# Weights times v in an attention and two-layer kernel: the second head's matmul goes first in each turn of the two heads

## The chip, the cores and the metric

One core of a Trainium2 chip runs the whole program. The metric is the device time of one execution in microseconds. An execution that was recorded by the profiler gives the rows that are shown below; its own time stands beside the times of the runs without a profile.

## What is computed

The reference is attention with a causal mask and a bias from cumulated gates, followed by two feed-forward layers:

```python
scores = scale * q @ k.T                       # 4 batches, 8 heads, 576 positions, 64 wide
bias = -(cum[:, None] - cum[None, :])          # cum: running sum of max(s, 0)
scores = where(causal, -1e9, scores + minimum(bias, 0))
attn = exp(scores - max(scores)); attn = attn / (sum(attn) + 1e-9)
x = attn @ v                                   # then (2304, 512)
x = max(x @ w1, x @ w2, x @ w3) @ w_out        # 512 -> 768 -> 512
x = ((x @ w_a) * (x @ w_b)) @ w_out2           # 512 -> 1536 -> 512
```

The change touches `attn @ v` alone. Everything is float32.

## The kernel before

Two heads are worked on together as a pair, and the 576 query positions of a batch are cut into a part of 256 (R = 0) and one of 320 (R = 1). That gives 4 x 2 x 4 = 32 pairs. For each pair the scores go to PSUM, VectorE adds the mask and finds the maximum (line 367), ScalarE takes the exponential (line 374), GpSimd divides by the sum (line 383), and TensorE transposes the weights in pieces of 128 x 128 (`f_t0` at line 476 for R = 0; `t_unit` and `t_joint` at lines 512, 514 and 525 for R = 1). ScalarE copies the transposes from PSUM into the tile `PF` (lines 479, 517, 520, 526), whose second index is the head.

Then `f_pv` (lines 481 to 502) multiplies by v. The result of a pair is one PSUM tile `fpv` of 128 partitions: the first head writes partitions 0 to 63, the second 64 to 127. Each matmul has a stationary operand of 128 x 64, so the first head's matmuls use columns 0 to 63 of the array and the second head's columns 64 to 127. For R = 0 each head has two matmuls, of 256 and 128 columns; for R = 1 it has five, of 320, 320, 320, 192 and 64. They are float32, and in the trace each stands as two records of that many columns. The list `mm` holds them by head, and the loop at lines 495 and 496 takes one of each head in turn. ScalarE and VectorE then read the tile (`f_x`, lines 506 and 507) and write `Xh` and `Xl`, the input of the first feed-forward layer. All 32 sets of matmuls together are called the 32 groups below: 16 shorter ones (R = 0) and 16 longer ones (R = 1).

The order on each engine is not the order in the code. The program is written as a stream of small pieces (pieces of attention, units of the first feed-forward layer `gate` at line 553 and `outp` at line 580, weight loads `load_w1`), each with a priority (`tc.high_priority`). A scheduler then plans the program with times of its own and puts on an engine what has the priority among those instructions that it holds to be ready. So a matmul of line 498 whose operand it holds to be late is passed by others, such as gates of the first layer. Instructions on TensorE are executed in the order that the scheduler wrote. The second feed-forward layer (line 951) follows from 530 us on and has no part in the attention.

The copy of the second head's transposes comes last in a pair: `f_t0` is called for head 0 and then head 1 (line 667), and in R = 1 the last piece is `do_t(2, 1)` (line 689).

Of the kernel before, what the change touches and what calls it, by code (L numbers as in the profile page):

```python
# [27 lines left out]
def kernel(  # L28
# [175 lines left out]
    def pt4(t, h):  # L204
        return t[:, h].rearrange("p (j c) -> p j c", c=N1)
# [275 lines left out]
    def f_pv(R, PF, vn):  # L481
        n = Q0 if R == 0 else N1
        ps = ps_t.tile([P, 512], F32, tag="t", name="fpv")
        mm = []
        for h in range(2):
            hs = slice(h * D, h * D + D)
            if R == 0:
                m = [(vn[:, 0, hs], PF[:, h, 0:256], 0), (vn[:, 1, hs], PF[:, h, 256:384], P)]
            else:
                m = [(vn[:, j, hs], pt4(PF, h)[:, j], 0) for j in range(3)]  # L490
                m.append((vn[:, 3, hs], pt4(PF, h)[:, 3, P:], P))
                m.append((vn[:64, 4, hs], PF[:64, h, 3 * N1 : 3 * N1 + 64], 256))
            mm.append(m)

        for t in range(len(mm[0])):
            for h in range(2):
                w, x, c0 = mm[h][t]
                nc.tensor.matmul(  # L498
                    ps[h * D : h * D + D, c0:n], w, x,
                    start=(t == 0), stop=(t == len(mm[h]) - 1),  # L500
                )
        return ps
# [129 lines left out]
    def attn_pieces(i, X):  # L632
# [10 lines left out]
        def pv():  # L643
            f_x(R, p, f_pv(R, st["PT"], nat_of.pop(i)[2]), *X())
            ahead(i + 2)
# [643 lines left out]
```

## Time and profile before

| what | value |
|---|---|
| median of 3 runs | 975.48 us (974.85 to 976.46) |
| the profiled execution's own time | 977.47 us |
| its span, from the first to the last instruction | 975.7 us |
| TensorE (PE) busy | 927.9 us, 95% of the span |
| VectorE busy | 618.5 us, 63% |
| ScalarE busy | 397.7 us, 41% |
| GpSimd busy | 276.6 us, 28% |
| line 498 on PE | 73.7 us busy in its largest group of instructions, 432 records |

The table has one execution. Busy time of PE counts a matmul from its start to its modelled end; since matmuls overlap in the array, the distance from one start to the next tells what an instruction costs, and the views in order of time give the starts. A row in order of time that ends in x18 holds 18 instructions that follow each other.

### The profile page before, as it was taken

The page shows a single profiled execution, that of the slowest core. Times are in us where ns is not written, and L with a number is a line of the kernel's source. Part 1 is how long each engine was busy: PE and PEld are TensorE (multiplying, and loading weights), DVE is VectorE, ACT ScalarE, POOL GpSimd, SP SyncE. Part 2 cuts the span into 40 slices and gives each one's busy share as a digit, 9 for nine tenths or more (in the row PEclk, how much of TensorE's full clock was granted, in tenths as well). Part 3 has the DMA queues.
Part 4 walks back from the last instruction along what each step waited for, and adds up shares of the span by engine and source line. Part 5 has one row for each costly group of instructions (what it writes and reads, how often), then busy time and mean ns, then how long its engine had stood idle before and what let it go on. Part 6 is the DMA issues. An engine that isn't in the chain of part 4 may idle for free.

```text
span 975.7 us, 17008 instructions
## 1 busy us (share of the span) xinstructions
PE 927.9 (95%) x6182; PEld 849.9 (87%) x6182; DVE 618.5 (63%) x1404; ACT 397.7 (41%) x902; POOL 276.6 (28%) x379
## 2 busy tenths in 40 slices
PE   5899999999999999999999789999999999599998
PEld 4576689988998889988889789999999999599998
DVE  5999623544344543454291888887877579868774
ACT  4766733555446554465431422232322233233231
POOL 6676522232233222333241212111111111212210
PEclk9999999999999999999999979999999999799999
DMA  5555241313223132220130524444443121552531
GB/s 168 191 183 164 89 107 53 92 39 103 57 79 91 40 91 68 80 81 29 60 115 22 195 76 135 151 152 151 145 136 100 57 98 57 159 169 89 172 109 44
DMA packets 55211, 102.34 MB, mean 105 GB/s; under 512 B 5736, under 2 KB 39432, under 8 KB 55128
## 3 DMA queue, kind: packets, MB, share of 16 engines
q1 hardware_dynamic: 55128, 101.26, 32.9%
q8 instruction: 49, 0.80, 0.4%
q14 instruction: 34, 0.28, 0.1%
HBM read 77.29 MB, written 23.94 MB: 104 GB/s over the span
## 4 chain that ended last, share of the span: by engine, by line
PE 66%; DVE 13%; DMA 13%; issue 3%; POOL 1%; ACT 1%; SPq 1%; POOLq 0%; DVEq 0%; ACTq 0%
PE g L553 20%; PE X L951 14%; PE Z L951 7%; PE o L580 7%; PE fpv L498 6%; PE Y L951 3%; DMA wraw<-in_moe_w_out_dram 3%; PE t L512 2%; DVE u L838 2%; DMA wraw<-in_moe_w_b_dram 2%; DVE wl L838 2%; PE s L390 1%; DMA qvraw<-in_qv_dram 1%; PE s L391 1%; DMA wraw<-in_moe_w_a_dram 1%
## 5 line engine op out<-in xcount | busy, mean ns | idle before, releaser
L553 PE MATMUL g<-Xh,hg 128*128 128x256 f32 (+1 forms) x576 | 174.5, 305 | 4.0 <-ACT xo L585 2.4
L553 PE MATMUL g<-Xl,hg 128*128 128x256 f32 (+1 forms) x576 | 174.4, 303 | 0.9 <-DVE rs L378 0.9
L553 PE MATMUL g<-Xh,lg 128*128 128x256 f32 (+1 forms) x576 | 174.2, 303 | 0.0
L553 PEld LDWEIGHTS g<-Xh,hg 128*128 128x128 f32 x576 | 109.3, 190 | 9.6 <-issue 3.3
L553 PEld LDWEIGHTS g<-Xl,hg 128*128 128x128 f32 x576 | 109.8, 191 | 4.0 <-issue 2.1
L553 PEld LDWEIGHTS g<-Xh,lg 128*128 128x128 f32 x576 | 109.7, 191 | 4.0 <-issue 3.5
L951 PE MATMUL X<-xh,wh 128*128 128x384 f32 x288 | 99.3, 345 | 7.5 <-ACT u L986 3.0
L86 POOL TENSOR_SCALAR wh<-wval 128x256 fp32r<-128x256 f32 x84 | 43.7, 531 | 200.4 <-PE Z L951 128.2
L951 PE MATMUL X<-xl,wh 128*128 128x384 f32 x288 | 97.9, 340 | 1.0 <-DVE xl L838 1.0
L951 PE MATMUL X<-xh,wl 128*128 128x384 f32 x288 | 98.0, 340 | 0.3 <-DVE wl L838 0.3
L951 PE MATMUL X<-woh,slot 128*128 128x256 f32 x432 | 83.0, 285 | 6.8 <-ACT slot L79 6.3
L562 DVE TENSOR_TENSOR hf<-g,hf 128x256 f32<-128x256 f32 (+1 forms) x96 | 43.6, 455 | 64.0 <-PE g L553 53.5
L838 DVE TENSOR_TENSOR slot<-hraw,slot 128x768 fp32r<-128x768 f32 x63 | 63.1, 1024 | 21.7 <-POOL slot L86 18.7
L951 PEld LDWEIGHTS X<-woh,slot 128*128 128x128 f32 x432 | 69.7, 193 | 7.3 <-ACT slot L79 6.7
L498 PE MATMUL fpv<-PF,qvraw 128*64 128x320 f32 (+4 forms) x432 | 73.7, 376 | 0.0
L383 POOL TENSOR_SCALAR P<-P,rs 128x128 f32<-128x128 f32 (+2 forms) x80 | 48.9, 616 | 71.2 <-DVE rs L379 47.8
L90 POOL TENSOR_TENSOR hl<-hf,hh 128x256 fp32r<-128x256 f32 (+1 forms) x48 | 40.7, 847 | 98.7 <-ACT hh L79 98.4
L951 PEld LDWEIGHTS X<-xh,wh 128*128 128x128 f32 x288 | 54.5, 189 | 12.1 <-ACT u L986 3.9
L86 POOL TENSOR_SCALAR slot<-hraw 128x768 fp32r<-128x768 f32 x27 | 27.3, 1010 | 129.5 <-DVE hraw L838 54.8
L374 ACT ACTIVATE P<-P,nm 128x128 f32<-128x128 f32 (+2 forms) x80 | 46.4, 581 | 38.1 <-DVE nm L367 34.8
L951 PE MATMUL X<-wol,slot 128*128 128x256 f32 x216 | 61.3, 285 | 0.0
L498 PEld LDWEIGHTS fpv<-PF,qvraw 128*64 128x64 f32 (+1 forms) x432 | 32.7, 137 | 31.6 <-issue 13.0
(158 smaller groups left out, 2370.1 us busy)
## 6 DMA issues: line engine op xcount, KB each, us to landing
hT<-u SPq DMA_DIRECT2D x72, 192.0 KB
hraw<-hT SPq DMA_DIRECT2D x36, 384.0 KB
wraw<-in_moe_w_dram SPq DMA_DIRECT2D x18, 512.0 KB
wraw<-in_moe_w_out_dram SPq DMA_DIRECT2D x18, 512.0 KB
qvraw<-in_qv_dram SPq DMA_DIRECT2D x12, 640.0 KB
kraw<-in_kT_dram SPq DMA_DIRECT2D x24, 288.0 KB
wraw<-in_moe_w_a_dram SPq DMA_DIRECT2D x12, 512.0 KB
wraw<-in_moe_w_b_dram SPq DMA_DIRECT2D x12, 512.0 KB
```

What stands on the lines that cost most here:

```text
L86: nc.gpsimd.tensor_scalar(o, i, scale, 1.0, op0=ALU.mult, op1=ALU.mult)
L90: e.tensor_tensor(o, a, b, op=ALU.subtract)
L374: nc.scalar.activation(pt[:, c0:c1], pt[:, c0:c1], AF.Exp, bias=first, scale=-1.0, accum_out=sm[:, g : g + 1],)
L383: nc.gpsimd.tensor_scalar(pt[:, c0:c1], pt[:, c0:c1], rs[:, g : g + 1], 1.0, op0=ALU.mult, op1=ALU.mult,)
L390: nc.tensor.matmul(ps, QA1[:, qs], KB1[:, h, ksl], start=True, stop=False)
L498: nc.tensor.matmul(ps[h * D : h * D + D, c0:n], w, x, start=(t == 0), stop=(t == len(mm[h]) - 1),)
L512: nc.tensor.transpose(ps[:, j * P : j * P + P], pt[:, j * P : j * P + P], ident)
L553: nc.tensor.matmul(ps[:, :n], w[:, kk, :], x[:, kk, :], start=(i == 0), stop=(i == len(mm) - 1),)
L562: nc.vector.tensor_tensor(hf, ps[:, :n], hf, op=ALU.max)
L580: nc.tensor.matmul(ps[:, :n], w[:, c, :], x[:, m, :n], start=(i == 0), stop=(i == len(mm) - 1),)
L838: {"V": nc.vector, "P": nc.gpsimd}[e].tensor_tensor(o, a, b, op=op)
L951: nc.tensor.matmul(ps[:, :n], w, x, start=(first and i == 0), stop=(i == len(mm) - 1), skip_group_check=not first,)
```

## The change

In the loop of `f_pv` over the two heads, the second head's matmul of each turn is written ahead of the first head's:

```diff
         for t in range(len(mm[0])):
-            for h in range(2):
+            for h in (1, 0):
                 w, x, c0 = mm[h][t]
                 nc.tensor.matmul(
                     ps[h * D : h * D + D, c0:n], w, x,
                     start=(t == 0), stop=(t == len(mm[h]) - 1),
                 )
```

An empty line is added above the loop, so each line behind it has a number higher by one in the changed kernel (498 becomes 499, 553 becomes 554). The matmuls, their operands and their results are the same 224 as before. What changes is the order that the scheduler writes.

The first place is TensorE at a longer group late in the attention, `fpv_5355`. Before, around the group's first matmul (`t2` is a transpose of the second head's weights, `g` a gate matmul of the first layer):

```order
L553 MATMUL g_5195<-Xh_4466,hg_1_1_124 128x256
L553 MATMUL g_5195<-Xl_4467,hg_1_1_124 128x256
L512 MATMUL t2_5334<-ident_81,P2_5292 128x128 x3
L498 MATMUL fpv_5355<-PF_5174,qvraw_4938 64x320
L553 MATMUL g_5195<-Xh_4466,lg_1_1_125 128x256
L553 MATMUL g_5195<-Xh_4466,hg_1_1_124 128x256
L553 MATMUL g_5195<-Xl_4467,hg_1_1_124 128x256
```

and 23 rows later the rest of the same group (`s3` are scores of the next pair):

```order
L553 MATMUL g_5261<-Xh_4466,hg_0_2_128 128x256
L553 MATMUL g_5261<-Xl_4467,hg_0_2_128 128x256
L498 MATMUL fpv_5355<-PF_5174,qvraw_4938 64x320 x5
L498 MATMUL fpv_5355<-PF_5174,qvraw_4938 64x192 x2
L498 MATMUL fpv_5355<-PF_5174,qvraw_4938 64x64 x2
L390 MATMUL s3_5447<-KB1_112,QA1_114 128x512
```

Now the whole group stands in one place:

```order
L554 MATMUL g_5245<-Xh_4466,lg_2_1_127 128x256
L554 MATMUL g_5245<-Xh_4466,hg_2_1_126 128x256
L499 MATMUL fpv_5355<-PF_5174,qvraw_4938 64x320 x6
L499 MATMUL fpv_5355<-PF_5174,qvraw_4938 64x192 x2
L499 MATMUL fpv_5355<-PF_5174,qvraw_4938 64x64 x2
L390 MATMUL s3_5447<-KB1_112,QA1_114 128x512
L391 MATMUL s3_5447<-KB2_113,QA2_115 128x512
```

The group's first matmul, the first head's, stood apart from the other nine; now all ten follow each other, at the place where the nine stood, ahead of the same scores.

The second place is a shorter group, `fpv_4619`, on TensorE. Before (`s0` are scores of a later pair):

```order
L553 MATMUL g_4476<-Xl_3667,hg_0_1_122 128x320
L498 MATMUL fpv_4619<-PF_4491,qvraw_4312 64x256
L553 MATMUL g_4476<-Xh_3666,lg_0_1_123 128x320
L390 MATMUL s0_4680<-KB1_112,QA1_114 128x256
L553 MATMUL g_4476<-Xh_3666,hg_0_1_122 128x320
L391 MATMUL s0_4680<-KB2_113,QA2_115 128x256
L553 MATMUL g_4476<-Xl_3667,hg_0_1_122 128x320
L390 MATMUL s0_4680<-KB1_112,QA1_114 128x256
L553 MATMUL g_4476<-Xh_3666,lg_0_1_123 128x320
L391 MATMUL s0_4680<-KB2_113,QA2_115 128x256
L553 MATMUL g_4510<-Xh_3666,hg_1_1_124 128x320
L498 MATMUL fpv_4619<-PF_4491,qvraw_4312 64x256
```

Now:

```order
L554 MATMUL g_4510<-Xl_3667,hg_1_1_124 128x320
L554 MATMUL g_4510<-Xh_3666,lg_1_1_125 128x320
L499 MATMUL fpv_4619<-PF_4491,qvraw_4312 64x256 x2
L499 MATMUL fpv_4619<-PF_4491,qvraw_4312 64x128 x2
L554 MATMUL g_4510<-Xh_3666,hg_1_1_124 128x320
L554 MATMUL g_4510<-Xl_3667,hg_1_1_124 128x320
```

One matmul of 256 columns stood nine rows ahead of the other three; now the four stand together.

The third place is the start of the program, around `fpv_446` on TensorE (`ft0` are transposes of the next pair, `f2`, `f3` scores of later ones). Before:

```order
L553 MATMUL g_928<-Xh_273,hg_0_0_116 128x256
L553 MATMUL g_972<-Xh_273,hg_1_0_118 128x256
L498 MATMUL fpv_446<-PF_373,kqv_172 64x256 x2
L498 MATMUL fpv_446<-PF_373,kqv_172 64x128 x2
L553 MATMUL g_928<-Xl_274,hg_0_0_116 128x256
L553 MATMUL g_928<-Xh_273,lg_0_0_117 128x256
```

Now:

```order
L554 MATMUL g_986<-Xh_273,lg_2_0_121 128x256
L499 MATMUL fpv_446<-PF_373,kqv_172 64x256
L476 MATMUL ft0_510<-ident_81,F0_463 128x128
L476 MATMUL ft0_515<-ident_81,F0_479 128x128
L476 MATMUL ft0_510<-ident_81,F0_463 128x128
L499 MATMUL fpv_446<-PF_373,kqv_172 64x256
L476 MATMUL ft0_515<-ident_81,F0_479 128x128
L476 MATMUL ft0_510<-ident_81,F0_463 128x128
L499 MATMUL fpv_446<-PF_373,kqv_172 64x128
L476 MATMUL ft0_515<-ident_81,F0_479 128x128
L499 MATMUL fpv_446<-PF_373,kqv_172 64x128
L434 MATMUL f2_560<-kraw_277,qvraw_278 128x384
```

Here the group was in one piece, and now transposes stand between all of its four matmuls.

Over the whole program, the groups stand so on TensorE (a piece is a row of line 498's matmuls with nothing between them):

| | groups in one piece | in two | in three | in four | in five | pieces in all |
|---|---|---|---|---|---|---|
| before | 2 | 27 | 2 | 1 | 0 | 66 |
| now | 28 | 0 | 1 | 2 | 1 | 44 |

Before, the two whole groups are `fpv_446` and `fpv_1962`, those in three pieces `fpv_650` and `fpv_787`, and that in four `fpv_1811`. Now four of the first five groups are in pieces: `fpv_268` in three, `fpv_446` and `fpv_528` in four, `fpv_650` in five; `fpv_359` and all groups from the sixth on stand whole. From `fpv_1962` on, the kernel before has 12 longer groups and 8 shorter ones in two pieces each. In the second layer a few short stretches of matmuls change places with their neighbours.

## Rows read from the trace of the kernel before

**Rows 1.** Busy us by stretch: length, PE, PEld, DVE, ACT, POOL; then clock, DMA share, GB/s.
```profile
0.00:50.00 50.00, 37.35 (x176) 26.54 (x176) 37.07 (x106) 29.90 (x77) 31.69 (x44) 0.97 0.60 179
50.00:100.00 50.00, 47.52 (x304) 34.12 (x303) 47.15 (x105) 34.00 (x76) 34.91 (x32) 1.00 0.52 165
...
150.00:485.00 335.00, 334.15 (x2413) 298.23 (x2412) 146.85 (x486) 168.13 (x420) 99.02 (x144) 1.00 0.23 66
485.00:600.00 115.00, 103.87 (x606) 100.20 (x605) 83.81 (x148) 33.05 (x64) 29.06 (x40) 0.94 0.32 108
```

**Rows 2.** All waits of PE from 150 to 485 us: engine, line, releaser, us, times, longest.
```profile
PE ft L476 <- POOL P L383: 0.4, 2, 0.2
```

**Rows 3.** PE in order of time at 453 us: start us, us, what runs.
```profile
453.17 0.60 PE L512 MATMUL t<-ident,P 128*128 128x128 f32 x4
...
453.73 0.28 PE L553 MATMUL g<-Xh,lg 128*128 128x256 f32 x1
```

**Rows 4.** PE in order of time around a longer group, 442 to 450 us.
```profile
442.77 0.49 PE L512 MATMUL t<-ident,P 128*128 128x128 f32 x3
443.19 0.75 PE L498 MATMUL fpv<-PF,qvraw 128*64 128x320 f32 x2
443.87 0.39 PE L553 MATMUL g<-Xh,lg 128*128 128x256 f32 x1
444.09 0.28 PE L553 MATMUL g<-Xh,hg 128*128 128x256 f32 x1
...
447.01 2.42 PE L498 MATMUL fpv<-PF,qvraw 128*64 128x320 f32 x18
449.35 0.50 PE L390 MATMUL s<-KB,QA 128*128 128x512 f32 x1
```

**Rows 5.** PE in order of time around a shorter group, 377 to 381 us.
```profile
377.32 0.31 PE L553 MATMUL g<-Xh,hg 128*128 128x320 f32 x1
377.47 0.31 PE L553 MATMUL g<-Xl,hg 128*128 128x320 f32 x1
377.71 0.65 PE L498 MATMUL fpv<-PF,qvraw 128*64 128x256 f32 x2
378.28 0.41 PE L553 MATMUL g<-Xh,lg 128*128 128x320 f32 x1
378.54 0.28 PE L390 MATMUL s<-KB,QA 128*128 128x256 f32 x1
...
379.69 0.86 PE L498 MATMUL fpv<-PF,qvraw 128*64 128x256 f32 x6
380.48 0.42 PE L553 MATMUL g<-Xl,hg 128*128 128x320 f32 x1
```

**Rows 6.** PE in order of time at 157 us, a shorter group in one piece.
```profile
157.25 0.87 PE L498 MATMUL fpv<-PF,qvraw 128*64 128x256 f32 x8
158.05 0.41 PE L553 MATMUL g<-Xh,hg 128*128 128x320 f32 x1
```

**Rows 7.** PE in order of time, 142 to 145 us, a shorter group in four pieces.
```profile
141.95 0.31 PE L553 MATMUL g<-Xh,hg 128*128 128x320 f32 x1
142.19 0.65 PE L498 MATMUL fpv<-PF,qvraw 128*64 128x256 f32 x2
...
145.35 0.31 PE L553 MATMUL g<-Xh,lg 128*128 128x320 f32 x1
```

**Rows 8.** Waits of PE up to 150 us.
```profile
PE f L434 <- DMA kraw<-cs: 9.3, 1, 9.3
PE g L553 <- ACT Xh L79: 1.6, 1, 1.6
...
PE f L434 <- DMA kraw<-ck: 1.1, 2, 0.7
```

**Rows 9.** ScalarE in order of time: the second head's copy before the body of rows 4.
```profile
443.43 0.45 ACT L517 COPY PF<-t 128x384 f32<-128x384 f32 x1
```

**Rows 10.** Tile fpv, weight loads: count, then ns shortest/median/longest.
```profile
L498 PEld LDWEIGHTS fpv<-PF,qvraw x432: 128/136/230, 22.3 to 481.0; 128*64 128x64 f32 x123, 64*64 64x64 f32 x21
```

## Prediction

> **What bounds the kernel now.** I read the busy time by stretch first. From 150 to 485 us PE is busy 334.15 of 335.00 us, at a granted clock of 1.00 (its 2.4 GHz level), while DVE has 146.85, ACT 168.13 and POOL 99.02 us of work and the DMA engines are busy 23% of the time [rows 1]. The view of PE's waits agrees: 0.4 us in all of that stretch [rows 2]. So there the time is what TensorE's instructions cost one after the other, and an instruction that leaves its queue shortens the run by its whole cost. The start is different: in the first 100 us PE is busy 37.35 + 47.52 us, DVE is busy 37.07 and 47.15 us [rows 1], and apart from 9.3 us before the first matmul PE waits another 15.1 - 9.3 = 5.8 us, 1.6 us of them at one place [rows 1, 8]. From 485 to 600 us PE lacks 115.00 - 103.87 = 11.1 us [rows 1].
>
> Then I read PE in order of time, since busy times overlap and only the distance from one start to the next is a cost.
>
> **What a piece costs.** The order of the changed kernel shows that the change does one thing to nearly all groups: the first head's first matmul, which stood apart, goes back to its group. Two prices are needed, that of the piece where it stands and that of the same matmul inside the group.
>
> *Longer group, standing apart.* From the first of three transposes (442.77) over the piece (443.19) to the second gate behind it (444.09) are 1.32 us [rows 4]. Without a piece, four transposes and the first gate take 453.73 - 453.17 = 0.56 us [rows 3]; a fourth transpose adds 0.60 - 0.49 = 0.11 us [rows 3, 4], so three take 0.45 us. The piece costs 1.32 - 0.45 = 0.87 us.
>
> *Shorter group, standing apart.* From the gate at 377.47 to the scores at 378.54 are 1.07 us; two gates at 0.15 us each (377.32 to 377.47) would take 0.30 us. The piece costs 0.77 us [rows 5]. Of the 0.77 us, 0.57 lie between the piece's start and the next (377.71 to 378.28), and 0.20 are extra distance ahead of it and behind it [rows 5].
>
> *The matmuls alone.* The longer group's piece has 0.68 us from its start to the next one (443.19 to 443.87), the shorter one's 0.57 us. The 0.11 us between them are two records of 64 more columns, so 0.86 ns per column and record: 320 columns are 2 x 320 x 0.86 = 0.55 us, 256 are 0.44, 128 are 0.22 [rows 4, 5]. What is left of 0.77 us, 0.33, is the price of leaving and re-entering this form of matmul.
>
> *Inside the group.* A shorter group without its first matmul takes 380.48 - 379.69 = 0.79 us for six records [rows 5]; the one whole group in the bound stretch takes 158.05 - 157.25 = 0.80 us for all eight [rows 6]. Merged, the matmul costs 0.01 us: the two heads use different columns of the array and run side by side. No row shows a whole longer group. Its body without the first matmul takes 449.35 - 447.01 = 2.34 us [rows 4]; by 0.86 ns the second head's five matmuls need 2 x 1216 columns = 2.09 us and the first head's four 2 x 896 = 1.54 us, together 3.63. So they do overlap, and the first head's side has 0.55 us to spare, just the merged matmul. The bounds are 0 us (as the shorter group shows) and 0.55 us (no overlap at all); I take 0, the value of the nearest row, and keep the other for the range.
>
> **The sum.**
> - 150 to 485 us: 12 longer pieces at 0.87 and 8 shorter at 0.77 us (the counts are from the order) go: 10.4 + 6.2 = 16.6 us.
> - 100 to 150 us: the group in four pieces takes 145.35 - 141.95 = 3.40 us with five gate steps of 0.15 [rows 7, 5], so 2.65; whole it would take 0.80 + 0.20 = 1.00 [rows 6, 5]. That is 1.65 us. Another shorter piece is 0.77 us. Behind two more, PE then waits for rows of `kraw`, 1.1 us in all and up to 0.7 each [rows 8]; of their 0.87 + 0.77 us I count 1.64 - 1.1 = 0.5, since the transfer does not come earlier. Together 2.9 us.
> - Up to 100 us: four of the first five groups are now in more pieces. `fpv_268` gets one more (0.33); `fpv_446` three more, and its matmuls no longer run side by side (3 x 0.33 + 0.44 + 0.22 = 1.65); `fpv_528` two more and one matmul alone (0.66 + 0.22 = 0.88); `fpv_650` two more and one more of 320 columns alone (0.66 + 0.55 = 1.21). Lost: 4.1 us. `fpv_787` loses two pieces (0.87 + 0.33) and `fpv_943` one (0.87): 2.1 us gained. `fpv_359` I count at nothing, since PE waits 1.6 us for `Xh` right behind it [rows 8]. Net a loss of 2.0 us.
>
> 16.6 + 2.9 - 2.0 = 17.5 us. The profiled execution took 977.47 us, which gives 960.0; it stands 2.0 us above the median of the runs, 975.48, so the median becomes **958.0 us**.
>
> What else moves: the gate, score and transpose matmuls are the same ones in another order. Transposes are now more often between gates; that costs nothing, as four of them and a gate take 0.56 us, 0.11 each and 0.12 for the gate [rows 3, 4]. The groups end where they ended, ahead of the same instructions, so `f_x` and what reads `Xh` and `Xl` come no later in PE's order; buffers (`PF`, v) are let go at the same place, and the loads behind them on SP's queue keep their distance. DVE, ACT and POOL cover their unchanged work as long as they stay under PE's time; with 17 us less in 335 the nearest, ACT, goes from 50% to 53%.
>
> **A rule against it.** The piece has two weight loads, of 136 ns each at the median [rows 10]; in the whole shorter group two more loads cost 0.01 us with their matmuls [rows 5, 6], so they are hidden. The Trainium skill, page "TensorE: Matmul & The Clock Gate", Part 3 on packing small matmuls, section "The mechanism", says that a weight load overlaps with running matmuls only where the row group differs; the two heads use the same rows and differ in columns. By that rule, the two loads of each merged matmul would be added to its group, and the time would be rival 2's instead of 958.0. The rows of the shorter group speak against it.
>
> **The rivals.**
> 1. *The start costs more.* The scheduler rewrote the first 100 us most; PE could wait there for weights that DVE, almost full there, converts later in the new order. For it: DVE's 47.15 of 50 us. Against it: PE's other waits there are only 5.8 us now. If new waits of 4 to 10 us come, the time is 962 to 968 us.
> 2. *The loads of merged matmuls are not hidden* (the mechanism that the rule names). 20 merged matmuls x 2 x 0.136 us = 5.4 us: 963.5 us. If longer groups did not overlap at all, 12 x 0.55 = 6.6 us: 964.6 us.
> 3. *Given back behind 485 us.* If the 11.1 us that PE lacks there hang on transfers that do not move, they grow; half of the gain lost is 967 us. Against it: those chains begin at the end of the attention, which moves with PE.
> 4. *Slower: PE stands at the head of the group.* The piece was work that could be done while the second head's copy was under way; now all waits for that copy. In rows 9 it ends at 443.43 + 0.45 = 443.88, 3.1 us before the body's start at 447.01 [rows 4, 9], and the whole group stands where the body stood, so no wait is expected. It decides where the copy comes over 3.1 us later; the run becomes slower where it comes 3.1 + 0.9 = 4.0 us later on the mean of the 20 groups. At 4.5 us: 20 x (4.5 - 4.0) = 10 us more than now, 985 us.
> 5. *Nothing happens*, 975.5 us: the two orders of a turn are mirror images, and if the order on PE were otherwise the same there would be nothing to gain. The order shows 66 pieces before and 44 now, which speaks against it.
>
> **How the numbers follow.** My forecast, 954 to 962 us, has 0.66; rival 1 has 0.13, rival 2 0.06, rival 3 0.05, rival 4 0.03, rival 5 0.02, and 0.05 go to a start that gains as well (net +2 instead of -2 us, and the 2 us or more that fewer waits there give: 952 to 954). Over 966 us lie rivals 4 and 5, most of 3 and a third of 1, about 0.13, and under 953 about 0.04, so the range is 953 to 966 us. A change within 0.2% (2 us) is about what a measurement of this kernel can't tell from none. Faster by more than that: 0.94 (all but rivals 4 and 5 and 0.01 of rival 3). Within: 0.03 (that and rival 5). Slower: 0.03 (rival 4).
>
> **What would show it.** In PE's order of time, groups of 20 records (longer) and 8 (shorter) at 2.3 and 0.8 us with no x2 piece ahead of them behind 100 us; their time in the page's group of line 499 falls; PE still shows under 1 us of waits between 150 us and the end of the attention, and the attention's last group starts some 17 us earlier. A group of 20 at 2.6 us says rival 2, at 2.9 no overlap. PE waiting for line 517's or 479's copies says rival 4. An attention that ends 17 us earlier in a run that isn't 17 us shorter says rival 3. The prediction is wrong if the pieces are gone and the stretch from 150 us to the attention's end is not shorter by 14 us or more.

## The result and the profile after

The changed kernel takes **960.25 us** at the median of 4 runs (957.59 to 961.97); the kernel before took 975.97 us on the same chip (4 runs, 974.85 to 976.61). The ratio is 0.9838, with a 95% interval of 0.9813 to 0.9863: 15.7 us less, where 17.5 us less had been forecast. The profiled execution took 960.02 us with a span of 958.2 us; the span before was 975.7 us.

The busy time by stretch of the changed kernel, cut 15 us earlier at the end of the attention than in [rows 1] (length, PE, PEld, DVE, ACT, POOL; then clock, DMA share, GB/s):

```profile
0.00:50.00 50.00, 36.72 (x161) 24.51 (x162) 35.59 (x106) 29.24 (x75) 31.16 (x44) 0.97 0.60 177
50.00:100.00 50.00, 46.20 (x302) 34.88 (x300) 45.16 (x99) 33.42 (x72) 34.65 (x30) 0.97 0.52 166
100.00:150.00 50.00, 46.70 (x317) 38.34 (x317) 21.90 (x80) 24.76 (x71) 17.33 (x25) 0.97 0.30 83
150.00:470.00 320.00, 319.50 (x2431) 296.94 (x2430) 149.12 (x499) 169.42 (x430) 103.68 (x150) 1.00 0.25 73
470.00:585.00 115.00, 105.55 (x625) 101.28 (x624) 85.11 (x153) 33.95 (x65) 33.64 (x42) 0.96 0.34 115
```

The same view of the kernel before, for the one stretch that [rows 1] leaves out:

```profile
100.00:150.00 50.00, 48.92 (x324) 40.37 (x324) 20.55 (x85) 26.11 (x76) 17.40 (x29) 1.00 0.40 108
```

From 150 us to the end of the attention PE is still full, at a granted clock of 1.00. Up to 150 us it is less busy than before: 36.72 + 46.20 + 46.70 = 129.62 us against 37.35 + 47.52 + 48.92 = 133.79 us, so it stands idle 4.2 us longer, and the clock is 0.97 in the second and third stretch, where it was 1.00.

PE's waits from 150 to 470 us are one row, as in [rows 2]:

```profile
PE t L513 <- POOL P L383: 0.5, 1, 0.5
```

A longer group in PE's order of time, where [rows 4] had a piece and a body of 18:

```profile
432.67 0.28 PE L554 MATMUL g<-Xh,lg 128*128 128x256 f32 x1
432.79 0.28 PE L554 MATMUL g<-Xh,hg 128*128 128x256 f32 x1
432.99 2.42 PE L499 MATMUL fpv<-PF,qvraw 128*64 128x320 f32 x20
435.35 0.50 PE L390 MATMUL s<-KB,QA 128*128 128x512 f32 x1
```

A shorter one, where [rows 5] had a piece and a body of 6:

```profile
370.81 0.31 PE L554 MATMUL g<-Xh,lg 128*128 128x320 f32 x1
371.05 0.87 PE L499 MATMUL fpv<-PF,qvraw 128*64 128x256 f32 x8
371.85 0.42 PE L554 MATMUL g<-Xh,hg 128*128 128x320 f32 x1
```

All instructions of line 499 with this operand, from the view by line (busy, mean ns of one, idle before), which had 73.7 us before:

```profile
L499 PE MATMUL fpv<-PF,qvraw 128*64 128x320 f32 (+4 forms) x432 | 56.9, 383 | 0.4 <-ACT PF L479 0.4
```

All 20 records of the longer group take 435.35 - 432.99 = 2.36 us, where 18 took 2.34; all 8 of the shorter take 0.80 us, where 6 took 0.79. Every group from 125 us on stands like these two, with no piece ahead of it.

The attention's last longer group, after and before:

```profile
464.45 2.42 PE L499 MATMUL fpv<-PF,qvraw 128*64 128x320 f32 x20
466.81 0.39 PE L581 MATMUL o<-hh,lo 128*128 128x256 f32 x1
```

```profile
478.85 2.42 PE L498 MATMUL fpv<-PF,qvraw 128*64 128x320 f32 x18
481.20 0.39 PE L580 MATMUL o<-hl,ho 128*128 128x256 f32 x1
```

It starts 14.4 us earlier. Where the 17.47 us between the two spans arise is read from three distances of the two traces. The first of the twelve longer groups of the bound stretch (its body, before) starts at 181.44 us before and at 184.55 us after: **3.1 us lost** up to there. From it to the last one are 478.85 - 181.44 = 297.41 us before and 464.45 - 184.55 = 279.90 us after: **17.5 us gained**. From the last one to the end are 496.8 us before and 493.8 us after: **3.1 us gained**.

Only the middle distance is firm. It is 278.90 to 280.44 us in all nine traces, this one and eight below, in which all twenty groups of that stretch stand whole and the heads alternate. The first distance changes from one execution to the next: the same changed kernel, run once more, has the group at 187.36 us, and a kernel whose order is that of before up to that group (the late pairs alone) has it at 183.38 and, once more, at 184.36 us, where before had 181.44. So of the 3.1 us lost no more than a part is shown to be the change's. The last distance, too, is 493.75 us in a kernel that keeps the pieces (all turns but the first), so the 3.1 us gained are not shown to be the change's either.

What the start of the changed kernel loses is seen in PE's waits up to 150 us, to be read against [rows 8]:

```profile
PE f L434 <- DMA kraw<-cs: 9.0, 1, 9.0
PE f L434 <- DMA kraw<-ck: 3.2, 1, 3.2
PE g L554 <- ACT Xh L79: 2.2, 1, 2.2
PE f L434 <- DVE nm L367: 1.9, 1, 1.9
PE f L434 <- DMA kqv<-cs: 1.7, 1, 1.7
```

Four rows are longer than before: `kraw<-ck` 3.2 (1.1), `Xh` 2.2 (1.6), `nm` 1.9 (0.2) and `kqv` 1.7 (0.9 us). Together they are 5.2 us longer; others are shorter, and the idle time grows by 4.2 us. The largest, in PE's order of time:

```profile
114.55 0.49 PE L513 MATMUL t<-ident,F 128*128 128x128 f32 x3
118.27 1.12 PE L434 MATMUL f<-kraw 66*128 66x128 f32 x4 [3.23 <-DMA kraw<-ck]
119.32 3.84 PE L499 MATMUL fpv<-PF,qvraw 128*64 128x320 f32 x20
123.08 0.49 PE L434 MATMUL f<-kraw 66*128 66x128 f32 x2
```

After 3.23 us without work, a whole longer group of 20 records takes 123.08 - 119.32 = 3.76 us, not 2.35. The granted clock of those 4 us (118 to 122 us):

```profile
118.00:122.00 4.00, 3.73 (x14) 1.75 (x16) 1.50 (x8) 1.91 (x9) 2.88 (x6) 0.60 0.16 61
```

0.60 is a mean in which most of the stretch is at the 1.2 GHz level. The kernel before has 1.00 in the same four microseconds:

```profile
118.00:122.00 4.00, 3.64 (x25) 3.02 (x26) 2.15 (x14) 3.22 (x13) 2.86 (x5) 1.00 0.13 34
```

So another 1.4 us went in the group behind the wait of 3.2 us.

Why the row of `kraw` comes late is seen on SP's queue, first after, then before (start us, us, what is issued):

```profile
109.81 0.33 SPq L307 DMA_DIRECT2D qvraw<-in_qv_dram  x1
110.52 0.33 SPq L217 DMA_DIRECT2D wraw<-in_moe_w_out_dram  x1
111.47 0.32 SPq L292 DMA_DIRECT2D kraw<-in_kq_dram  x1
115.61 0.55 SPq L305 DMA_DIRECT2D kraw<-ck  x1
```

```profile
105.38 0.34 SPq L307 DMA_DIRECT2D qvraw<-in_qv_dram  x1
106.60 0.32 SPq L292 DMA_DIRECT2D kraw<-in_kq_dram  x1
109.76 0.55 SPq L305 DMA_DIRECT2D kraw<-ck  x1
```

The load of the next v (line 307) needs the buffer of a v that a group on PE still reads. That group ends at 109.70 us now (PE's next matmul) and ended at 105.27 us before; the load is issued 0.11 us behind it in both. What stands behind it on SP's queue moves along, the load of the extra rows of `kraw` (line 305) by 115.61 - 109.76 = 5.85 us. Of these, 4.43 us are the later group; the rest lies between the two loads, where a load of `wraw` (line 217) has come in and line 305 stands 4.14 us behind line 292, not 3.16. The wait of SP for that line is 8.2 us at its longest now, 5.8 before:

```profile
SPq L307 <- PE fpv L499: 10.2, 2, 8.2
```

```profile
SPq L307 <- PE fpv L498: 5.8, 1, 5.8
```

The kernel with the first turn alone (below) speaks for this place on the queue as the cause of the wait. Its group of 20 records ends as late, at 109.97 us, but there the scheduler wrote the load of v behind that of `kraw`:

```profile
107.18 0.32 SPq L292 DMA_DIRECT2D kraw<-in_kq_dram  x1
110.52 0.54 SPq L305 DMA_DIRECT2D kraw<-ck  x1
111.16 0.35 SPq L307 DMA_DIRECT2D qvraw<-in_qv_dram  x1
```

It has no such wait, a granted clock of 1.00 from 118 to 122 us, and the next group, at 118.39 us, takes 2.36 us; its first longer group of the bound stretch starts at 181.13 us.

### The profile page after: what moved, and what is told of

Its sections match the earlier page's. It is cut to its first block, busy times and chain, and to the rows that moved or that the text cites. A ratio compares the mean times of both kernels' runs of the same rounds, so it can differ in the third digit from the quotient of the medians.

```text
span 958.2 us, 16985 instructions
## 1 busy us (share of the span) xinstructions
PE 908.4 (95%) x6182; PEld 844.5 (88%) x6182; DVE 617.7 (64%) x1404; ACT 396.8 (41%) x902; POOL 284.0 (30%) x379
## 4 chain that ended last, share of the span: by engine, by line
PE 68%; DVE 13%; DMA 11%; issue 3%; POOL 2%; ACT 1%; SPq 1%; ACTq 0%; DVEq 0%; POOLq 0%
PE g L554 21%; PE X L952 15%; PE Z L952 7%; PE o L581 7%; PE fpv L499 5%; PE Y L952 3%; DMA wraw<-in_moe_w_out_dram 3%; PE t L513 2%; DMA wraw<-in_moe_w_b_dram 2%; DVE u L839 2%; DVE wl L839 2%; PE s L390 1%; DMA xt<-x2T 1%; PE s L391 1%; PE f L434 1%
## 5 line engine op out<-in xcount | busy, mean ns | idle before, releaser
L581 PE MATMUL o<-hh,ho 128*128 128x256 f32 (+1 forms) x192 | 57.8, 307 | 1.3 <-DVE hf L563 0.8
L79 ACT ACTIVATE slot<-hraw 128x768 fp32r<-128x768 f32 x36 | 30.4, 848 | 68.3 <-DVE hraw L839 35.9
```

The costliest lines, as they stand in the source:

```text
L79: nc.scalar.activation(o, i, AF.Copy, scale=scale)
L581: nc.tensor.matmul(ps[:, :n], w[:, c, :], x[:, m, :n], start=(i == 0), stop=(i == len(mm) - 1),)
```

## The experiments

The theory was that a piece costs PE 0.87 us (longer group) or 0.77 us (shorter), that the order of the two heads in the first turn alone decides whether there is one, and that the merged matmul costs nothing. The rivals were that the loads of merged matmuls or the waits of the start take part of it back, and that something else than the pieces is what shortens the run. Ratios are to the kernel before on the same chip, with 95% intervals.

**The first turn alone, and all turns but the first.** Two kernels on one chip (before: 977.7 us there).

```diff
-            for h in range(2):
+            for h in ((1, 0) if t == 0 else (0, 1)):
```

> Only the first turn of each group has the second head first; the later turns keep the old order. Theory (the gain is that the group's first matmul no longer stands apart): the order on PE has 44 pieces at the places of the changed kernel, so about 960 us (958 to 962). Rival (the order within every turn matters, say for the array's columns): 966 to 976 us.

Measured: 958.73 us (957.51 to 959.35), ratio 0.9805 (0.9786 to 0.9825).

```diff
-            for h in range(2):
+            for h in ((0, 1) if t == 0 else (1, 0)):
```

> The mirror image: the first turn keeps the old order, all later turns have the second head first. Theory: 67 pieces, one more than before, so the time of before, 976 us (974 to 978). Rival (the order within every turn matters): 960 to 970 us.

Measured: 974.87 us (972.49 to 980.12), ratio 0.9976 (0.9958 to 0.9994). The first turn carries all of the gain; turning the others around brings 0.2%, about what a measurement can tell from no change. Both came out as the theory expected. The rival that the new order is better by itself falls.

**The late pairs alone** (on the same chip): the old order up to the twelfth pair, the new one from the thirteenth on, which is the stretch where PE is full.

```diff
-    def f_pv(R, PF, vn):
+    def f_pv(R, PF, vn, late=True):
...
-            for h in range(2):
+            for h in ((1, 0) if late else (0, 1)):
...
-            f_x(R, p, f_pv(R, st["PT"], nat_of.pop(i)[2]), *X())
+            f_x(R, p, f_pv(R, st["PT"], nat_of.pop(i)[2], i >= 12), *X())
```

> The second head goes first from the 13th pair on; the first twelve pairs are written as before, and their order on PE is that of before. This is the term of 16.6 us by itself: 976 - 16.6 = 959.4 us, with the first 150 us as before. Rival (the stretch behind 150 us gives some 20 us, as the changed kernel's trace suggests by being 3.7 us late at 150 us and 17.5 early at the end): 955 to 957 us.

Measured: 956.44 us (955.57 to 958.45), ratio 0.9786 (0.9765 to 0.9808). From the first to the last of the twelve longer groups are 462.64 - 183.38 = 279.26 us, 18.2 less than before. The time is 3 us below the 959.4 of the sum and within the rival's range, but the stretch gives 18.2 us, not the rival's 20; the first group starts 1.9 us later than before and the end comes 5.7 us sooner behind the last one, which no term foresaw. The stretch that was predicted best carries the gain; that the change of the first twelve pairs adds to it is not seen. Busy time from 100 to 150 us in this kernel, and its wait for `kraw`:

```profile
100.00:150.00 50.00, 48.58 (x317) 39.12 (x316) 22.03 (x87) 26.82 (x79) 17.34 (x28) 1.00 0.38 103
```

```profile
PE f L434 <- DMA kraw<-ck: 1.1, 1, 1.1
```

With the old order at the start the wait is the old 1.1 us and the clock the old 1.00.

**All groups whole** (on the same chip): the change, and a priority that keeps each group together, so that only 32 pieces are left where the change has 44.

```diff
-            f_x(R, p, f_pv(R, st["PT"], nat_of.pop(i)[2]), *X())
+            with tc.high_priority(400):
+                ps = f_pv(R, st["PT"], nat_of.pop(i)[2])
+            f_x(R, p, ps, *X())
```

> The change, and a priority higher by 400 for the matmuls with v, so that all 32 groups stand whole, those of the start too. Theory (pieces cost PE time at the start as well): against the changed kernel 268 saves 1.1, 446 and 528 1.65 each and 650 2.4 us, together 6.8: 960.25 - 6.8 = 953.5 us. Rival (the start hangs on VectorE and on loads, and pieces there cost nothing): 959 to 962 us.

Measured: 957.19 us (956.89 to 958.79), ratio 0.979 (0.9768 to 0.9812): about 1.5 us less than the first turn alone beside it, not the 6.8 expected. The view by stretch shows what stands against it:

```profile
0.00:50.00 50.00, 35.18 (x156) 26.13 (x157) 35.17 (x102) 28.88 (x75) 29.98 (x43) 0.90 0.59 176
50.00:100.00 50.00, 45.91 (x303) 36.37 (x303) 46.70 (x102) 33.51 (x74) 33.90 (x30) 0.93 0.51 168
100.00:150.00 50.00, 46.70 (x316) 38.24 (x314) 20.48 (x78) 24.45 (x68) 17.15 (x26) 0.93 0.29 79
```

PE is busy 127.79 us in the first 150 us, 6.0 us less than before, and what it does there it does at granted clocks of 0.90 to 0.93. Its wait for `kraw` is 3.3 us, as in the change. In this trace, work that is taken from PE where PE is not the bound became waiting, and behind the waits stands a lower clock.

**One kind of group each.** Before took 975.88 us on the chip of these runs.

```diff
-            for h in range(2):
+            for h in ((1, 0) if R else (0, 1)):
```

> Second head first in the longer groups (R = 1) alone; 51 pieces. By the prices of the pieces: behind 150 us 12 x 0.87 = 10.4 us go and one shorter group gets a second piece (0.8 back); up to 150 us the longer groups lose four pieces (0.88 + 0.87 + 0.87 + 0.87) and one shorter group two (0.9). 976 - 14 = 962 us, with 2 us either way for the start. Rival (one kind of group carries nearly all of the gain): 958 to 960 or over 968 us.

Measured: 968.68 us (968.3 to 970.25), ratio 0.9921 (0.9893 to 0.9949): 7.2 us, a miss by 6.7, and by its number in the rival's range of over 968 us. But one kind does not carry nearly all of the gain, as the stretch shows here and in the next run. Between the first and the last longer group it gains what was expected of it: 287.94 us against 297.41, 9.5 us for 11 pieces, where 11 x 0.87 = 9.6. Up to the first of them it is 4.1 us later than before, where a gain had been expected, in part as in the changed kernel:

```profile
114.98 1.68 PE L434 MATMUL f<-kraw 66*128 66x128 f32 x8 [1.56 <-DMA kraw<-ck]
116.60 4.07 PE L498 MATMUL fpv<-PF,qvraw 128*64 128x320 f32 x20
120.60 0.55 PE L476 MATMUL ft<-ident,F 128*128 128x128 f32 x3
```

The wait for `kraw` is followed by a group of 4.00 us. I had also missed that one early shorter group goes to four pieces in this kernel.

```diff
-            for h in range(2):
+            for h in ((1, 0) if R == 0 else (0, 1)):
```

> Second head first in the shorter groups (R = 0) alone; 61 pieces. Behind 150 us 8 x 0.77 = 6.2 us go; up to 150 us two groups gain 2.4 us and five get more pieces, a loss of some 4 us. 976 - 4.8 = 971 us, with 2 us either way. Together with the run of the longer groups alone the gains should add up to about that of the changed kernel. Rival as there.

Measured: 964.91 us (964.2 to 968.21), ratio 0.9886 (0.9854 to 0.9917): 11.0 us, a miss on the other side, outside of both ranges. In the same stretch it takes 287.44 us, 10.0 less than before, where 8 x 0.77 = 6.2 had been worked out. Sixteen gate and output matmuls fewer lie in the stretch by the trace's records, at some 0.14 us each from one to the next 2.2 us, so the eight pieces are worth about 7.7 us, nearly 1 us each. In the stretch the two halves sum to 19.4 us against the 17.5 of the whole change; corrected in the same way for the matmuls that lie elsewhere (7 more in the one, 16 fewer in the other, 4 fewer in the change) they are 10.4 + 7.7 = 18.1 against 17.0.

**From which pair on.** The edit of the late pairs, with `i >= 8` and `i >= 5` (on the same chip).

> Second head first from the 9th pair on; 41 pieces, the first eight pairs as before. Against the run from the 13th pair on (956.4 us) two shorter groups more stand whole, one of them in four pieces so far: 0.77 + 1.65 = 2.4 us, so 954 us. Rival (up to 150 us pieces cost nothing since PE waits for loads there): 956 to 957 us.

Measured: 955.38 us (952.54 to 957.63), ratio 0.9789 (0.9751 to 0.9827). This lies between the 954 of the theory and the rival's 956 to 957, and its runs cover both.

> Second head first from the 6th pair on; 40 pieces, the first five pairs as before. Against the run from the 13th pair on (956.4 us) three longer groups and one shorter one more stand whole, and one stays in four pieces: 1.2 + 0.87 + 0.87 + 0.77 = 3.7 us less, 952.7 us, if PE bounds the stretch from 50 to 150 us. Rival (that stretch waits for loads, and faster groups only wait longer): 955 to 958 us.

Measured: 959.38 us (955.94 to 961.74), ratio 0.982 (0.9785 to 0.9854). This is above the 952.7 expected and the 955 to 958 of the rival; that the sixth to eighth pairs would add to the gain is not seen: with them the time is 4 us longer, by the medians.

**The heads one after the other.** The second head's five (or two) matmuls, and then the first head's. There is no piece behind 170 us here either, so this tells the effect of the pieces from that of two heads side by side. Before took 976.38 us on this chip.

```diff
-        for t in range(len(mm[0])):
-            for h in range(2):
+        for h in (1, 0):
+            for t in range(len(mm[0])):
```

> The second head's matmuls of a group all come first, then all of the first head's; the same matmuls, none of them in a piece of its own behind 150 us. Theory (two matmuls run side by side only where the two heads' matmuls stand next to each other in PE's order): a longer group takes some 1.3 to 1.8 us more than the changed kernel's 2.35 (2 x 2.09 us of columns less the 2.35 gives 1.8 as the upper end), a shorter one 0.3 to 0.6 more than 0.80; with some 12 longer and 9 shorter groups in the steady stretch that is 18 to 27 us there, and in all about 985 us (978 to 995): slower than the kernel before, though there are no pieces. Rival (the pieces alone decide; the array overlaps matmuls of two column groups however far apart they stand): 2.35 and 0.80 us as in the changed kernel, 958 to 962 us.

Measured: 996.17 us (993.7 to 997.77), ratio 1.0192 (1.016 to 1.0224), slower than the kernel before by 19.8 us and just above the 978 to 995 us expected. The rival, that the pieces alone decide, is out. A longer and a shorter group in PE's order of time:

```profile
211.05 4.75 PE L498 MATMUL fpv<-PF,qvraw 128*64 128x320 f32 x20
215.73 0.39 PE L553 MATMUL g<-Xh,lg 128*128 128x256 f32 x1
```

```profile
272.87 0.88 PE L498 MATMUL fpv<-PF,qvraw 128*64 128x256 f32 x8
273.68 0.42 PE L553 MATMUL g<-Xl,hg 128*128 128x320 f32 x1
```

The longer group takes 4.68 us; the second half of its records starts 2.34 us behind the first and takes as long: the heads no longer run side by side at all. Between the first and the last of the twelve longer groups are 307.82 us, 28.0 more than in the trace of the change on the same chip (below), where 11 x 2.33 = 25.6 would be the groups' own; that is most of the 37.5 us between the two medians. The price of 1.3 to 1.8 us was too low. The shorter group, against my expectation, loses nothing (0.81 us).

**Once more, on one chip**: the change, and the two versions that had lower medians (before: 976.38 us, the same runs as for the heads one after the other).

> The change once more, beside the two versions of this call on the same chip: 958 to 961 us.

Measured: 958.65 us (6 runs, 957.09 to 963.46), ratio 0.9808 (0.9782 to 0.9835). Its wait up to 150 us is the same again:

```profile
PE f L434 <- DMA kraw<-ck: 2.9, 1, 2.9
```

> The change from the ninth pair on, once more. If its 955.4 us is a property of the order (the early pieces keep PE's work where waits for converted weights would stand anyhow), it is again 3 to 5 us below the change: 955 to 957 us. If it was the scatter of starts, it is within 2 us of the change.

Measured: 955.62 us (6 runs, 951.71 to 958.33), ratio 0.9778 (0.975 to 0.9806), at the near end of the 3 to 5 us expected below the change.

> The change from the thirteenth pair on, once more. The order up to there is the old one, so the start costs what it cost before, and 16.6 us go from the steady stretch: 958 to 960 us by the sum; if the changed start costs 2 to 4 us more than the old one, it is 1 to 3 us below the change of this call.

Measured: 957.94 us (6 runs, 952.54 to 958.26), ratio 0.9792 (0.9764 to 0.9819): 0.7 us below the change, not the 1 to 3 us of a changed start that costs 2 to 4 us more.

The change from the ninth pair on has the lowest median on both of its chips, 3.0 us below the change on the same chip. The intervals overlap, and two of its six runs lie above the change's fastest, so it is the likelier best, not a shown one. By their medians both later starts are at least as good as the change, with fewer groups touched.

## Why the prediction was right, and where it was off

**What bounds the kernel** held. From 150 us on PE stays without waits, and what leaves its queue leaves the run.

**The merged matmul costs nothing**: 20 records take 0.01 to 0.02 us more than 18, and 8 take 0.01 us more than 6. The upper bound of 0.55 us and rival 2 are out. The rule that was weighed there (the Trainium skill, page "TensorE: Matmul & The Clock Gate", Part 3, section "The mechanism": a weight load overlaps only where the row group differs) is not what this trace shows: the two heads share their rows, differ in columns, and their loads stay hidden.

**The price of a piece and their number** gave 15.7 us between the first and the last longer group (11 x 0.87 + 8 x 0.77), and the trace shows 17.5, of which some 0.5 us are four output matmuls that lie elsewhere. So the terms were a little low, more for the shorter pieces than for the longer, as the two kernels with one kind of group show. A part of it is outside of line 499: summed from one start to the next, that line's cost in the stretch falls by 12.0 us and that of the transposes, next to which many pieces stood, by 4.6 us: a piece is paid for partly by its neighbours.

**The start** is the step that failed. It was sized at 2.9 us gained from 100 to 150 us and 2.0 lost before, net 0.9, and with the piece that stands ahead of the first longer group 1.8 us gained up to that group. The trace shows 3.1 lost and the repeat 5.9, against one trace of before. The sentence that was wrong is the one that loads behind the groups on SP's queue keep their distance. PE reaches the group that frees the v buffer 4.4 us later, the load waits for it, and the next rows of `kraw`, behind it on the queue, come 5.85 us later, so PE waits 3.2 us where all waits of this row came to 1.1, and runs its next group mostly at the 1.2 GHz level. In the repeat of the change the wait is 2.9 us; in the kernels that keep the old order up to there it is 0.4 to 1.5 us, and their gain is no smaller. What the start costs in all stays open: the first turn alone has no such wait and loses nothing up to the group (181.13 us), yet its ratio of 0.9805 is that of the change once more, 0.9808, and two starts of one order differ by up to 2.9 us.

**Behind the attention** nothing was predicted, and 3.1 us were gained in this trace; so the last group starts only 14.4 us earlier, not some 17, while the run is 17.5 us shorter. PE lacks 115.00 - 105.55 = 9.45 us in the 115 us behind the cut, where it lacked 11.1 [rows 1]; rival 3, which would have had them grow, is out. This gain and the loss at the start cancel in this pair of traces, so that the sum came nearer than its terms; that is luck.

**Rival 1** came in at its lower end: 4.2 us of new idle time up to 150 us, in waits for loads and for `nm`, not for the converted weights that it named, but larger terms elsewhere paid for it. **Rival 4**: waits of line 499 for the copies are 0.4 us in all, none behind 150 us. **Rival 5** is out by the result; the kernel with all turns but the first, where the pieces stay, shows what it had described, 974.87 us.

## What to carry to other kernels

When an engine is full, price the interruptions of a group of instructions, not only the instructions: here one early matmul that could start before its group cost 0.8 to 1 us each time, because it ran alone (inside the group it costs 0.01 us) and slowed its neighbours, and its result is read only when the whole group is done. With the operand first that comes last, the scheduler tore fewer groups apart: 28 of 32 stood whole here, where 2 had. Where the engine is not the bound (here the first 150 us) the same edit moves buffer releases and the loads that queue behind them, so try it from the point on from which the engine is full; here that was as good, by the medians.

## What the runs showed of the hardware

Two heads that use different columns of the array ran side by side, or not, by how far apart they stood in PE's order. Next to each other, 20 records took 2.35 us; with ten records of one head ahead of the other's, 4.68 us. With four records ahead (the shorter groups of that kernel) they still ran side by side, in 0.81 us: in the records the first two 256-column matmuls start 13 ns apart, though a matmul of 128 columns stands between them in the program. Where a gate stands between the two heads of such a group (at 166.93 and 168.06 us), each head's four records take 0.80 us by themselves, so the eight do overlap. The Trainium skill, page "TensorE: Matmul & The Clock Gate", Part 3, section "The mechanism", says that matmuls start and end strictly in program order; these records, which do not name the head, read otherwise. Where between four and ten records it ends was not tried.

A stall of PE of 3.2 us was followed by a stretch with a granted clock of 0.60 in which a group took 3.76 instead of 2.35 us. The cost of that wait, with the 1.4 us behind it, was nearly half as much again as the wait row shows.
